# One drain of GpSimd behind the seventh expert's last output scatter, in a fused attention and mixture-of-experts kernel

## Chip, cores and metric

The kernel runs on one core of one Trainium2 chip. The metric is the device time of one execution in microseconds. The kernel before took 474.51 us, the median of three runs (473.42 to 476.02).

## What is computed

Local and global attention over 8 batches and 8 heads (512 local tokens, 32 global ones, head size 64, a window of 32 to either side) gives 4352 token rows of 512 floats. A mixture of 8 experts follows: each row whose skip score is positive goes to the expert with the highest gate value, and the expert's output, times its gate weight, is added to the row. Rows that are not computed stay as they are.

```python
x = attn_out.transpose(0, 2, 1, 3).reshape(B * S, H * D)   # 4352 x 512
do_compute = x @ w_skip > 0
xc = x[do_compute]
e_idx = argmax(xc @ w_gate, axis=1)
gate_w = softmax(xc @ w_gate)[range(len(xc)), e_idx]
for e in range(E):                                         # 8 experts
    mask = e_idx == e
    h = maximum(xc[mask] @ w1[e], 0.0)                     # 512 -> 1024
    y[mask] = gate_w[mask, None] * (h @ w2[e])             # 1024 -> 512
out[do_compute] = xc + y
```

## The kernel before, in words

The first part (to about 235 us) is the attention, 32 pairs of heads in a hand-written order. It writes each finished row to `out` in DRAM, computes the routing, and with indirect DMAs that GpSimd issues (line 688) it scatters row number and gate weight into a list `lst` with one stretch for each expert.

The second part is the loop `for e in range(E)` at line 1041, unrolled, one turn for each expert. The order of the instructions on TensorE, VectorE, ScalarE, GpSimd and SyncE is the program's own (`tc.manual_schedule`, line 1014), so each engine takes its instructions in the order in which the code gives them. A turn for expert e, as far as GpSimd is in it:

- Line 1043: two indirect DMAs (line 119, in `gather`) fetch the expert's rows 256 to 511 from `out` into the tile `xmore`. They are issued whether there are that many rows or not. Then, for e from 1 to 6, two more (line 1049) fetch the first 256 rows of expert e+1 into `xfirst` or `xsecond`.
- Line 1078, `ffn`: 256 rows through both matrix products on TensorE. For the first 128 rows VectorE adds gate weight times result to the row (line 1007, tile `yo`) and GpSimd scatters them into `out` (line 1008, in `put`). The second 128 rows are kept back.
- Lines 1054 and 1083: each engine loads the expert's row count into a register and branches. Only where the count is over 256 are the rows in `xmore` computed. On the way around, the engines bring the semaphores up to what the skipped instructions would have made them; GpSimd does this for those of its DMAs with an instruction that the trace names INC_SWDGE_SEM.
- Line 1104, `leave()`: the second 128 rows are finished (line 1007, tile `ylast`) and scattered (line 1008).

In the unrolled program expert 7 (e = 7) is the last. The two gathers at its head, its two scatters and its branch are all that GpSimd issues behind the last scatter of expert 6. Behind the loop the framework closes the kernel; those instructions stand under line 1163 in the trace: SyncE waits for the semaphores one after the other, each engine executes an instruction named DRAIN and posts a semaphore, GpSimd waits for these posts, releases the engines, clears semaphores and drains again, and a second exchange of semaphores ends the program. Line 1153 holds the matching opening. Sequencer instructions (those whose engine name ends in q in the trace) do not count as busy time of an engine.

Of the kernel before, what the change touches and what calls it, by code (L numbers as in the profile page):

```python
# [25 lines left out]
E, F = 8, 1024  # L26
# [18 lines left out]
def kernel(  # L45
# [12 lines left out]
    nc = tc.nc  # L58
# [42 lines left out]
    def index(es, g):  # L101
        nc.vector.tensor_copy(six[:, es, g], lt[:, es, g, :, 0])

    def slots(es, g):
        if g == 0:
            nc.sync.dma_start(
                lt[:, es, 0].rearrange("p e t c -> p e (t c)"),
                l3[es, 0:GRP, :].rearrange("e (p t) c -> p e (t c)", t=NSUB),
            )
        else:  # L110
            for t in range(NSUB):
                nc.sync.dma_start(
                    lt[:, es, 1, t],
                    l3[es, GRP + t * P:GRP + (t + 1) * P, :].rearrange("e p c -> p e c"),
                )

    def gather(xg, gidx, nrow=NT):
        for t in range(NSUB):
            ins = nc.gpsimd.indirect_dma_start(  # L119
                out=xg[:, t, :], out_offset=None, in_=out[0:nrow, :],  # L120
                in_offset=bass.IndirectOffsetOnAxis(ap=gidx[:, t:t + 1], axis=0),
                bounds_check=nrow - 1, oob_is_err=False,
            )
            apart(ins, "gathers", "scatters")
# [3 lines left out]
    def tick(n=1):  # L128
        for _ in range(n):
            if stages:  # L130
                stages.pop(0)()

    def send_some(n):
        for _ in range(n):
            if sends:
                sends.pop(0)()
# [7 lines left out]
    def load_piece(e, eng=nc.sync):  # L144
        mine = raws.setdefault(e, {})
        i = len(mine)
        if i == PIECES:
            return
        at = (e - 1) * PIECES + i
        pool = early if e == 0 or at % 6 < 2 else stage  # L150
        raw = mine[i] = pool.tile([P, WC], F32, tag="raw", name="raw")
        j = i % (PIECES // 2)
        if i < PIECES // 2:
            eng.dma_start(raw, w1[e, j * P:(j + 1) * P, :])
        else:
            k = WC // DM
            eng.dma_start(
                raw.rearrange("p (c n) -> p c n", n=DM),
                w2[e, j * k * P:(j + 1) * k * P, :].rearrange("(c p) n -> p c n", p=P),
            )  # L160

    class Weights:
# [19 lines left out]
        def split(self, eng, parts=1):  # L182
            if self.done < parts * self.n:
                i, k = divmod(self.done, parts)
                self.done += 1
                sl = slice(k * WC // parts, (k + 1) * WC // parts)
                hi, lo, raw = self.view(i, "h")[:, sl], self.view(i, "l")[:, sl], self.raw[i][:, sl]
                nc.scalar.copy(hi, raw)
                eng.tensor_sub(lo, raw, hi.bitcast(F32))
# [11 lines left out]
    def turn_x(xg, i, nt=NSUB, bank=ps_t):  # L201
        xh, xl = xs[i]
        for t in range(nt):
            pt = bank("xt")
            for c in range(NC):
                nc.tensor.transpose(  # L206
                    pt[:, c * P:(c + 1) * P], xg[:, t, c * P:(c + 1) * P], ident
                )
            p3 = pt.rearrange("p (c n) -> p c n", n=P)
            ts_ = slice(t * P, (t + 1) * P)  # L210
            step = NC if nt > 1 else NC // 2
            for c in range(0, NC, step):
                nc.scalar.copy(xh[:, c:c + step, ts_], p3[:, c:c + step])  # L213
            nc.vector.tensor_sub(xl[:, :, ts_], p3, xh[:, :, ts_].bitcast(F32))
        return xh, xl
# [4 lines left out]
    with ExitStack() as actx:  # L220
# [549 lines left out]
        with tc.manual_schedule(engines=engines):  # L770
# [19 lines left out]
            for u in range(NU + 2):  # L790
# [73 lines left out]
                def after():  # L864
                    if u == NU - 2:
                        send_some(len(sends))
                        slots(first, 0)
                    if u == NU - 1:
                        tick(len(stages))
# [144 lines left out]
    with tc.manual_schedule(engines=engines | {mybir.EngineType.SP}):  # L1014
        def load_weights(e):
            weights[e] = Weights(e, *((w1b, w1b, w2b) if e % 2 else (w1a, v1a, w2a)))

        xgs = [xfirst, xsecond]
        x2 = x2[0]
        tick(13)  # L1020

        PARTS = [(slice(1, 2), 0), (slice(0, 1), 1), (slice(2, E), 0), (slice(1, E), 1)]

        def lists():
            send_some(len(sends))
            for es, g in PARTS:
                slots(es, g)
            nc.vector.tensor_sub(cnt, base[0:1, :], base0[0:1, :])
            nc.vector.tensor_copy(cni, cnt)  # L1029

        def rest():
            for es, g in PARTS[:2]:
                index(es, g)
            gather(xsecond, six[:, 1, 0, :])
            gather(xmore, six[:, 0, 1, :])
            for _ in range(4):
                weights[1].load(nc.gpsimd)
            for _ in range(2):
                load_piece(2, nc.gpsimd)

        for e in range(E):
            if e:
                gather(xmore, six[:, e, 1, :])
            if e + 1 < E:
                load_weights(e + 1)
                for _ in range(8 if e else 2):
                    weights[e + 1].load()
                if e:
                    gather(xgs[(e + 1) % 2], six[:, e + 1, 0, :])

            num, x2n = [], []

            def nxt():
                num.append(nc.values_load(cni[0:1, e:e + 1], min_val=0, max_val=CAP))  # L1054
                if e + 1 < E:
                    x2n.append(turn_x(xgs[(e + 1) % 2], (e + 1) % 2))

            def split():
                if e + 1 < E:
                    weights[e + 1].split(nc.vector)  # L1060

            if e == 0:
                todo = {i: split for i in (4, 5, 6, 7)}
                def after():
                    tick(len(stages))
                    lists()

                def others():
                    for es, g in PARTS[2:]:
                        index(es, g)  # L1070

                todo.update({1: after, 9: rest, 16: others, 22: nxt})
            else:
                todo = {i: lambda e=e: weights[e].split(nc.vector) for i in range(4)}
                todo.update({i: split for i in (4, 5, 6, 8)})
                todo[16] = nxt

            leave = ffn(
                e, x2, xgs[e % 2], lambda t, e=e: lt[:, e, 0, t, 1:2], six[:, e, 0, :],
                lambda i: todo.get(i, int)(), ps_v,  # L1080
            )
            num = num[0]
            with tc.If(num > GRP):  # L1083
                more = (
                    xmore, lambda t, e=e: lt[:, e, 1, t, 1:2], six[:, e, 1, :],
                )
                with tc.If(num > GRP + P) as big:  # L1087
                    ffn(e, turn_x(xmore, e % 2), *more)()
                    with tc.If(num > 2 * GRP):
                        with tc.For_i(2 * GRP, num, GRP) as i:  # L1090
                            lt2 = fw.tile([P, NSUB, 2], F32, name="lt2", bufs=1)
                            nc.sync.dma_start(
                                lt2.rearrange("p t c -> p (t c)"),
                                l3[e, ds(i, GRP), :].rearrange("(p t) c -> p (t c)", t=NSUB),
                            )
                            s2 = fw.tile([P, NSUB], U32, name="s2", bufs=1)
                            nc.vector.tensor_copy(s2, lt2[:, :, 0])
                            gather(xmore, s2)
                            ffn(
                                e, turn_x(xmore, e % 2), xmore, lambda t: lt2[:, t, 1:2], s2,  # L1100
                            )()
                with big.Else():
                    ffn_half(e, turn_x(xmore, e % 2, 1), *more)
            leave()
            x2 = x2n[0] if x2n else None


_INS = ["qT", "kT", "v", "vgl", "qgT", "w9", "w1", "w2"]
# [58 lines left out]
```

## Time and profile before

| what | us |
|---|---|
| median of three runs | 474.51 |
| range of these runs | 473.42 to 476.02 |
| the profiled execution's own time | 475.83 |
| its span, first to last instruction | 474.1 |
| granted TensorE clock, mean share of full speed | 0.975 |

TensorE is busy for 442.0 us of the span, VectorE for 303.2, ScalarE for 284.1 and GpSimd for 231.1. Times in the rows below count from the start of the span. A busy time of an engine leaves out the instructions that its sequencer handles alone, so a stretch in which no engine is busy has to be looked up among the sequencer instructions of a line.

### The profile page before, as it was taken

What the parts mean: (1) busy time and instruction counts of PE and PEld (TensorE: products, weight loads), DVE (VectorE), ACT (ScalarE), POOL (GpSimd) and SP (SyncE); (2) the same over time, 40 slices, a digit from 0 to 9 for tenths busy, and PEclk for the clock granted to TensorE, in tenths of its full rate; (3) what the DMA queues carried; (4) which work ended last, traced back from release to release, by engine and by line L of the source; (5) the groups of instructions that cost most, each with busy time, mean ns of one, the idle gap of its engine ahead of it and who ended that gap; (6) DMA issues with size and microseconds to landing.
All of it is one profiled execution on the core that took longest, in us unless ns stands there. A gap on an engine that the chain in (4) does not pass through costs nothing. (4 is left out here: it accounts for less than half of the span.)

```text
span 474.1 us, 13569 instructions
## 1 busy us (share of the span) xinstructions
PE 442.0 (93%) x4962; PEld 373.8 (79%) x4962; DVE 303.2 (64%) x1207; ACT 284.1 (60%) x867; POOL 231.1 (49%) x238
## 2 busy tenths in 40 slices
PE   8799999998899999799989999999999999999991
PEld 4677878786788777689869797989779898698980
DVE  6898888997778789866433184848317575166610
ACT  5699999998899988664412081818126272254500
POOL 7567777789966778874461050505005140042300
PEclk9799999999999999979989999999999999999997
DMA  7989998989998896413546056565604857037000
GB/s 257 294 295 320 300 314 313 304 303 295 294 272 259 199 319 159 133 47 99 104 103 243 24 187 239 178 255 179 252 1 145 301 166 295 3 119 246 25 18 17
DMA packets 50593, 93.32 MB, mean 197 GB/s; under 512 B 15644, under 2 KB 19996, under 8 KB 50496
## 3 DMA queue, kind: packets, MB, share of 16 engines
q1 hardware_dynamic: 44384, 80.78, 53.5%
q0 software_dynamic: 6112, 11.30, 7.1%
q8 instruction: 55, 0.90, 0.9%
q14 instruction: 42, 0.34, 0.3%
HBM read 82.91 MB, written 14.67 MB: 206 GB/s over the span
## 5 line engine op out<-in xcount | busy, mean ns | idle before, releaser
L398 ACT ACTIVATE prob<-prob,nmx 128x160 f32<-128x160 f32 x256 | 106.8, 423 | 15.4 <-DVE nmx L393 15.3
L435 POOL TENSOR_TENSOR prob<-prob,inv 128x640 f32<-128x640 f32 x64 | 80.6, 1261 | 33.1 <-DVE inv L431 18.3
L1008 POOL DMA_INDIRECT out_dram<-yo,six x12 | 12.2, 1017 | 126.8 <-DVE yo L1007 109.3
L931 ACT ACTIVATE hh<-ph 128x256 fp32r<-128x256 f32 x72 | 27.6, 384 | 66.8 <-PE ph L926 62.9
L942 PE MATMUL py<-w2h,hlw 128*128 128x512 f32 x144 | 56.6, 393 | 0.5 <-DVE hlw L932 0.5
L942 PE MATMUL py<-w2h,hh 128*128 128x512 f32 x144 | 57.0, 396 | 0.0
L942 PE MATMUL py<-w2l,hh 128*128 128x512 f32 x144 | 56.4, 392 | 0.0
L380 PE MATMUL pss<-ks,qs 64*64 64x160 f32 x1024 | 53.4, 314 | 0.9 <-DVE nmx L393 0.5
L398 ACT ACTIVATION_READ_ACCUMULATOR prob<-prob,nmx 128x1 f32 x256 | 49.5, 193 | 0.0
L539 PEld LDWEIGHTS pv<-ptT,vw 128*64 128x64 f32 x1024 | 41.9, 140 | 9.2 <-issue 8.6
L926 PE MATMUL ph<-xh,w1h 128*128 128x256 f32 x288 | 46.1, 282 | 2.5 <-ACT xh L213 0.8
L539 PE MATMUL pv<-ptT,vw 128*64 128x64 f32 (+1 forms) x1024 | 46.7, 240 | 0.0
L926 PE MATMUL ph<-xh,w1l 128*128 128x256 f32 x288 | 45.4, 280 | 0.0
L926 PE MATMUL ph<-xl,w1h 128*128 128x256 f32 x288 | 45.4, 280 | 0.0
L932 DVE SCALAR_TENSOR_TENSOR hlw<-ph,hh 128x256 fp32r<-128x256 f32 x72 | 30.2, 420 | 20.7 <-ACT hh L931 19.9
L380 PEld LDWEIGHTS pss<-ks,qs 64*64 64x64 f32 x1024 | 35.8, 138 | 9.4 <-issue 5.5
L926 PEld LDWEIGHTS ph<-xh,w1h 128*128 128x128 f32 x288 | 39.0, 189 | 4.9 <-issue 3.7
L688 POOL DMA_INDIRECT lst<-dat,slu x34 | 34.7, 1022 | 15.0 <-DVE cni L1029 6.3
L213 ACT CAST xh<-xt 128x512 fp32r<-128x512 f32 (+1 forms) x22 | 11.2, 551 | 50.2 <-PE xt L206 50.2
L476 PE MATMUL pst<-ident,prob 128*128 128x128 f32 x256 | 40.7, 286 | 0.0
L926 PEld LDWEIGHTS ph<-xl,w1h 128*128 128x128 f32 x288 | 38.8, 189 | 0.0
L926 PEld LDWEIGHTS ph<-xh,w1l 128*128 128x128 f32 x288 | 38.7, 189 | 0.0
(178 smaller groups left out, 970.2 us busy)
## 6 DMA issues: line engine op xcount, KB each, us to landing
raw<-in_w_dram SPq DMA_DIRECT2D x58, 512.0 KB, 6.1
vw<-in_v_dram SPq DMA_DIRECT2D x32, 512.0 KB, 7.1
ks<-in_kT_dram SPq DMA_DIRECT2D x32, 400.0 KB, 5.7
out_dram<-xr SPq DMA_DIRECT2D x32, 256.0 KB, 5.8
qs<-in_qT_dram SPq DMA_DIRECT2D x31, 256.0 KB, 5.9
raw<-in_w_dram POOLq DMA_DIRECT2D x6, 512.0 KB, 5.7
vgs<-in_vgl_dram SPq DMA_DIRECT2D x32, 64.0 KB, 5.5
lst<-dat,slu POOLq DMA_INDIRECT x34, 5.3
```

The costliest lines, as they stand in the source:

```text
L213: nc.scalar.copy(xh[:, c:c + step, ts_], p3[:, c:c + step])
L380: nc.tensor.matmul(banks[odd][head(h ^ odd), j * W:(j + 1) * W], q[head(h), w * QB:(w + 1) * QB], window(k[head(h)], w), start=True, stop= ...
L398: nc.scalar.activation(pt[:, i, :], pt[:, i, :], AF.Exp, bias=nmx[:, i:i + 1], scale=-1.0, accum_out=sums[:, i, 0:1],)
L435: nc.gpsimd.tensor_mul(pt[:, sl, :], pt[:, sl, :], inv[:, sl].unsqueeze(2).to_broadcast([P, 4, W]),)
L476: nc.tensor.transpose(pst[:, i * P:(i + 1) * P], pt[:, 4 * hf + i, 0:KW], ident)
L539: nc.tensor.matmul(pv[head(h), j * 96:j * 96 + n], vv[:, w, head(h)], ptT[:, w, h ^ odd, 0:n], start=False, stop=j == 3, skip_group_check= ...
L688: ins = nc.gpsimd.indirect_dma_start(out=lst, out_offset=bass.IndirectOffsetOnAxis(ap=slu[:, t:t + 1], axis=0), in_=dat[:, bs[j], t - 4 * ...
L926: nc.tensor.matmul(ph[:, 0:GRP], hl[a][:, c, f * P:(f + 1) * P], bb[:, c, :], start=i == 0, stop=i == 3 * NC - 1,)
L931: nc.scalar.activation(hh[:, f, :], ph[:, 0:GRP], AF.Relu)
L932: nc.vector.scalar_tensor_tensor(hlw[:, f, :], ph[:, 0:GRP], 0.0, hh[:, f, :].bitcast(F32), ALU.max, ALU.subtract,)
L942: nc.tensor.matmul(py, a[:, f, ts_], hl[bb][:, f, :], start=f == 0 and i == 0, stop=f == NF - 1 and i == 2,)
L1008: ins = nc.gpsimd.indirect_dma_start(out=out, out_offset=bass.IndirectOffsetOnAxis(ap=sidx, axis=0), in_=yo, in_offset=None, bounds_check= ...
```

## The change

One instruction is added to the loop over the experts: behind `leave()` of the turn with e = 6, GpSimd executes a drain. Nothing else differs.

```diff
             leave()
             x2 = x2n[0] if x2n else None
+            if e == E - 2:
+                nc.gpsimd.drain()
```

In GpSimd's order the drain stands between the scatter of `ylast` of expert 6 (line 1008) and the first gather of `xmore` of expert 7 (line 119).

## Rows read from the trace of the kernel before

**Rows 1.** The page: the span.
```profile
span 474.1 us, 13569 instructions
```
**Rows 2.** Sums by stretch: length, busy time (instructions) by engine, granted clock, DMA share, GB/s.
```profile
446.40:459.20 12.80, 12.80 (x84) 11.62 (x83) 5.83 (x10) 3.44 (x7) 0.00 (x0) 1.00 0.01 2
...
465.70:474.10 8.40, 0.00 (x0) 0.00 (x0) 0.00 (x0) 0.00 (x0) 0.00 (x0) 0.59 0.06 21
```
**Rows 3.** Timeline, 463 us to the end: start, length, engine, operation, idle before it.
```profile
463.23 0.39 PE L942 MATMUL py<-w2h,hlw 128*128 128x512 f32 x1
463.66 0.75 DVE L1007 SCALAR_TENSOR_TENSOR ylast<-py,lt,xsecond 128x512 f32<-128x512 f32 x1 [4.69 <-PE py L942]
464.69 1.00 POOL L1008 DMA_INDIRECT out_dram<-ylast,six  x1 [4.42 <-DVE ylast L1007]
```
**Rows 4.** Line 1008, the last scatter (464.69): issue to landing.
```profile
DMA to landing us min/median/max: 2.6/2.6/2.6
```
**Rows 5.** Line 1163 by time, 463 us on: ns min/median/max, first and last start.
```profile
L1163 DVEq DRAIN  x1: 791/791/791, 463.7 to 463.7; - x1
L1163 PEldq DRAIN  x1: 8/8/8, 463.8 to 463.8; - x1
L1163 POOLq DRAIN  x1: 8833/8833/8833, 464.5 to 464.5; - x1
...
L1163 SPq EVENT_SEMAPHORE  x9: 28/28/28, 467.3 to 467.8; - x9
L1163 SPq DRAIN  x2: 7/10/13, 467.9 to 467.9; - x2
...
L1163 POOLq EVENT_SEMAPHORE  x4: 17/17/17, 473.3 to 474.0; - x4
L1163 POOLq DRAIN  x2: 46/78/109, 473.5 to 473.9; - x2
```
**Rows 6.** The chain that ended last, its last piece: start, length, what.
```profile
464.45 1.24 POOLq L1163
```
**Rows 7.** GpSimd's semaphore instruction on the way around a branch, five of eight.
```profile
L1089 POOLq INC_SWDGE_SEM  x1: 1182/1182/1182, 273.0 to 273.0; - x1
...
L1083 POOLq INC_SWDGE_SEM  x1: 1266/1266/1266, 291.2 to 291.2; - x1
...
L1083 POOLq INC_SWDGE_SEM  x1: 1406/1406/1406, 315.0 to 315.0; - x1
...
L1083 POOLq INC_SWDGE_SEM  x1: 1930/1930/1930, 436.3 to 436.3; - x1
...
L1083 POOLq INC_SWDGE_SEM  x1: 2011/2011/2011, 460.1 to 460.1; - x1
```
**Rows 8.** DMA issues of GpSimd (POOLq), all of them: count, median us to landing.
```profile
raw<-in_w_dram POOLq DMA_DIRECT2D x6, 512.0 KB, 5.7
...
lst<-dat,slu POOLq DMA_INDIRECT x34, 5.3
...
xmore<-out_dram,six POOLq DMA_INDIRECT x16, 3.6
...
out_dram<-yo,six POOLq DMA_INDIRECT x12, 3.4
xfirst<-out_dram,six POOLq DMA_INDIRECT x8, 5.5
xsecond<-out_dram,six POOLq DMA_INDIRECT x8, 6.6
out_dram<-ylast,six POOLq DMA_INDIRECT x8, 2.7
```
**Rows 9.** Line 1153, the opening of the program: GpSimd's drain before any DMA.
```profile
L1153 POOLq DRAIN  x1: 183/183/183, 0.4 to 0.4; - x1
```
**Rows 10.** Timeline of GpSimd, 440 us on, without its last scatter.
```profile
442.07 1.00 POOL L1008 DMA_INDIRECT out_dram<-ylast,six  x1 [5.31 <-DVE ylast L1007]
443.37 1.05 POOL L119 DMA_INDIRECT xmore<-out_dram,six  x1 [0.30 <-issue]
444.73 1.63 POOL L119 DMA_INDIRECT xmore<-out_dram,six  x1 [0.31 <-issue]
459.25 1.02 POOL L1008 DMA_INDIRECT out_dram<-yo,six  x1 [12.89 <-DVEq L1083]
```
**Rows 11.** Line 1008, the scatter at 442.07: issue to landing.
```profile
DMA to landing us min/median/max: 2.8/2.8/2.8
```
**Rows 12.** Tile xmore, 430 us to the end: every instruction that touches it.
```profile
L119 POOL DMA_INDIRECT xmore<-out_dram,six x2: 1052/1339/1626, 443.4 to 444.7; - x2
```
**Rows 13.** Line 119, all gathers to 441 us: ns of one, and landing.
```profile
L119 POOL DMA_INDIRECT xmore<-out_dram,six x14: 994/1122/1636, 243.1 to 424.7; - x14
...
DMA to landing us min/median/max: 2.2/4.4/7.8
```

## Prediction

> **What bounds the kernel now.** I began with the page's span, 474.1 us [rows 1], and asked which work ends it. Up to 463 us it is TensorE: behind its last matmul at 463.23 VectorE finishes the last 128 rows at 464.41, and GpSimd issues their scatter from 464.69 to 465.69 [rows 3]. The scatter lands 2.6 us after its start, at 467.3 [rows 4]. After that nothing of the computation is left, yet the span goes on to 474.1: in the 8.4 us from 465.7 no engine is busy at all [rows 2]. A stretch like that has to be looked up among the sequencer instructions, and the chain of work names the line: its last piece is GpSimd's sequencer on line 1163, from 464.45 [rows 6].
>
> The instructions of that line, in order of time, are the heart of this case [rows 5]. The drains of TensorE and VectorE take 8 and 791 ns and are over by 464.5. SyncE has its last wait released by the landing at 467.3, steps through nine short waits, and its two drains begin at 467.9. GpSimd's drain takes 8833 ns: 464.45 + 8.83 = 473.28. The exchange of semaphores that ends the program starts at 473.3 and takes 474.1 - 473.3 = 0.8 us. So of the 6.8 us behind the landing, SyncE's steps explain 0.6 and the exchange 0.8. The 5.3 us between 467.9 and 473.3 belong to GpSimd's drain alone, with everybody else done.
>
> **Why that drain is long.** Three rows say what a drain costs when little stands before it: 183 ns at the opening, before any DMA [rows 9], and 109 and 46 ns for the two that follow the long one in the same closing [rows 5]. So a drain has no fixed price of 9 us. Nor is it the wait for the last transfer: it outlasts the landing by 473.28 - 467.3 = 5.98 us.
>
> The trace holds a second instruction whose length shows the same kind of growth. INC_SWDGE_SEM takes 1182 ns at 273 us, 1266 at 291, 1406 at 315, 1930 at 436 and 2011 at 460 [rows 7]. I set these against the DMAs that GpSimd has issued before each. All its issues are 6 + 34 + 16 + 12 + 8 + 8 + 8 = 92 [rows 8]; the last one comes behind the INC at 460, which so has 91 before it. Counting back through the program's order gives 87 at 436 us, 61 at 315, 55 at 291 and 49 at 273. The steps are 84 ns for 6, 140 for 6, 524 for 26 and 81 for 4: about 20 ns for each DMA in the last three, 829 / 42 = 19.7 over all. Time is not what it follows: 291 to 315 and 436 to 460 are both 23.8 us long, and the growth is 140 and 81 ns, with 6 and 4 DMAs. So in GpSimd's bookkeeping every DMA since the program's start still stands as an entry, though nearly all landed long ago, and some work of GpSimd's walks over them. The line's foot is 1182 - 49 x 19.7 = 217 ns.
>
> My reading is that a GpSimd drain settles those entries one by one and leaves the list empty. The price of an entry in a drain has two ends. If the walk over 92 begins with the landing it is 5.98 / 92 = 65 ns; if it begins behind the scatter's issue at 465.69 it is 7.59 / 92 = 83 ns. That the next drain takes 109 ns fits a list that was emptied.
>
> **The change, part by part.** It adds one instruction and removes and moves none.
>
> The added drain stands behind the scatter of expert 6, the one at 442.07 [rows 10], which leaves 92 - 4 = 88 entries (two gathers and two scatters come after it). From the scatter's landing, 442.07 + 2.8 = 444.87 [rows 11], 88 x 65 ns = 5.7 us give 450.6; from its issue end, 443.07, 88 x 83 ns = 7.3 us give 450.4. I take 450.6. Its shortest bound is the landing itself, 444.9; its longest comes from the load of the other engines, which the closing did not have: the second gather of `xmore` takes 1.63 us where the shortest takes 0.99 [rows 10, 13], a factor of 1.6, and 443.07 + 1.6 x 7.3 = 454.8.
>
> Queued behind it on GpSimd are the two gathers of `xmore` of expert 7, then the scatter at 459.25. The gathers now run from 443.15 to 446.36, 3.3 us behind the scatter's end; behind the drain they end at 450.6 + 3.3 = 453.9. What hides this is GpSimd's idle time: 12.89 us before the scatter at 459.25 [rows 10], in which TensorE is busy throughout [rows 2] and which ends with data from VectorE. There remain 459.25 - 453.9 = 5.3 us, and 1.1 us at the long bound. Nobody misses the gathers: after 430 us no instruction but the gathers themselves touches `xmore`, since expert 7 has no more than 256 rows [rows 12]. They must have landed before GpSimd goes around the branch, just before the INC at 460.1 [rows 7]: with the shortest landing, 2.2 us [rows 13], from the second one's start at 450.6 + 1.7 = 452.3, that is 454.5, and with the longest, 7.8 us, 460.1, a little late for the branch and 4 us ahead of the last scatter. SyncE has loads neither before nor behind in this stretch (2 GB/s are moved [rows 2]). Cost of the added drain: nothing.
>
> In the turn of expert 7 the INC_SWDGE_SEM at 460.1 finds 3 entries and not 91: about 217 + 3 x 20 = 0.28 us in place of 2.01. It gains nothing, since the last scatter waits for VectorE until 464.41 [rows 3].
>
> At the end, the framework's drain finds 4 entries. Behind the landing at 467.3 it needs 4 x 65 ns = 0.26, or, if it walked before, next to nothing: it ends between 467.3 and 467.6. Then SyncE is last, at 467.94, with its nine waits behind the same landing [rows 5]. The exchange, with about 0.05 to pass the signal, takes 0.85 us: 467.94 + 0.85 = 468.8. **The sum:** span 474.1 - 468.8 = 5.3 us less.
>
> The profiled execution took 475.83 us, 1.7 more than its span, and lies 1.3 above the median. What is saved lies inside the span, so I take it from each: 475.8 - 5.3 = 470.5 for that execution, 474.51 - 5.3 = **469.2** for the median.
>
> **What the Trainium skill says against it.** The row shows 8833 ns for GpSimd's drain in the closing and 7.6 us of it with the engine idle [rows 2, 5]. The Trainium skill, "PSUM — Partial Sum Buffer", section "Engine vs sequencer instructions", says that a drain waits for the engine to go fully idle, and names nothing else. By that rule alone the closing's drain would have ended at 465.7, and one more drain would save nothing. The trace disagrees by 7.6 us, but how entries are kept is told in no row, so the rule stands as the first rival below.
>
> **The rivals.** *The length does not depend on what is outstanding, or the drain does not empty the list.* The 5.98 us would be a price of the closing itself, paid again. For it: only one long drain is in the trace, and none is seen in the middle of work. Against it: the three short drains, and the line of INC_SWDGE_SEM. The added drain would then hide in the 12.89 us, as above, even at 8.83 us: 474.5. Here also belongs a drain that does not do what it says.
>
> *Part of it.* The drain is rid of the walk that INC_SWDGE_SEM shows, 92 x 20 ns = 1.8 us, and the other 4.1 us stay: 474.51 - 1.8 = 472.7, within 0.5%.
>
> *Slower: the drain outlasts its cover.* The place is GpSimd's queue from the drain to the last scatter. Behind the drain stand 3.3 us of gathers, 1.3 of the scatter of `yo` and its gap, and 2.0 of the INC [rows 7, 10]: 6.6 us. The last scatter waits for VectorE until 464.4, so it moves once the drain ends after 457.8, that is, after 14.7 us, twice the walk of 7.3. For it: GpSimd's work stretches under VectorE's load, by up to 1.6. Against it: 1.6 gives 454.8, and the gain in the closing would have to be lost as well. A drain of 20 us that empties nothing would end at 463.1 and give 474.5 + 5.3 = 479.8.
>
> **How the numbers follow.** Full gain 0.79 (469.2), part 0.05 (472.7), no effect 0.12 (474.5), slower 0.04 (479.8). Measurement tells about 0.5%, or 2.4 us, from no change. The full gain is 1.1%, so faster has 0.80 with a little of the partial cases, same 0.16, slower 0.04. For the range I take the full gain with the spread of the runs before, 1.1 below their median and 1.5 above, 468.1 to 470.7, and stretch it to the partial case, 472.7. It leaves out no effect and slower.
>
> **What would show it.** Right: a DRAIN of GpSimd of 7 to 9 us near 442 to 451, the gathers at about 451, INC_SWDGE_SEM at 460 of about 0.3 us, the closing's drain of about 3 us that ends with the landing, and SyncE's drain as the last before the exchange. Wrong: an INC still near 2 us (the list was not emptied), a closing drain still ending 6 us behind the landing, or the scatter of `yo` later than 459.3 (the cover did not hold).

## The result and the profile after

The changed kernel takes 468.26 us (median of four runs, 467.36 to 469.02) where the kernel before takes 474.45 beside it: ratio 0.9847, 95% interval [0.9812, 0.9882]. With 474.45 us that is 467.2 us, faster by 7.2 us or 1.5%. (The ratio is the comparison's own estimate and not the quotient of the two medians, which is 0.9870, or 6.2 us.) Forecast were 469.2 us and a gain of 5.3. The profiled execution took 467.36 us, with this span:

```profile
span 465.6 us, 13570 instructions
```

First the end of the timeline, as in [rows 3] (start, length, engine, operation, idle before it), and the last scatter's landing [rows 4]:

```profile
460.02 0.39 PE L942 MATMUL py<-w2h,hlw 128*128 128x512 f32 x1
460.44 0.75 DVE L1007 SCALAR_TENSOR_TENSOR ylast<-py,lt,xsecond 128x512 f32<-128x512 f32 x1 [4.69 <-PE py L942]
461.48 1.00 POOL L1008 DMA_INDIRECT out_dram<-ylast,six  x1 [4.42 <-DVE ylast L1007]
...
DMA to landing us min/median/max: 2.6/2.6/2.6
```

From the last matmul to the scatter nothing has changed but the place on the clock: all of it comes 3.2 us earlier than before. Then the closing, the line that was 1163 and is 1165 now, as in [rows 5], with the added drain (line 1107) ahead of it (ns min/median/max, first and last start):

```profile
L1107 POOLq DRAIN  x1: 8508/8508/8508, 438.7 to 438.7; - x1
...
L1165 POOLq DRAIN  x1: 3064/3064/3064, 461.2 to 461.2; - x1
...
L1165 SPq EVENT_SEMAPHORE  x9: 27/28/28, 464.1 to 464.6; - x9
L1165 SPq DRAIN  x2: 7/10/13, 464.7 to 464.7; - x2
...
L1165 POOLq EVENT_SEMAPHORE  x4: 17/17/17, 464.8 to 465.5; - x4
L1165 POOLq DRAIN  x2: 46/78/109, 464.9 to 465.3; - x2
```

GpSimd's closing drain has shrunk from 8.83 to 3.06 us. It ends at 461.24 + 3.06 = 464.30, 0.2 us behind the landing at 464.1, and SyncE, with its nine waits, is now the last, at 464.7. The exchange starts at 464.8. The long drain has not vanished: it stands at 438.7 and lasts 8.5 us. GpSimd's timeline shows what covers it, in the places of [rows 10]:

```profile
438.90 1.00 POOL L1008 DMA_INDIRECT out_dram<-ylast,six  x1 [5.31 <-DVE ylast L1007]
448.09 1.05 POOL L119 DMA_INDIRECT xmore<-out_dram,six  x1 [8.19 <-issue]
449.45 1.01 POOL L119 DMA_INDIRECT xmore<-out_dram,six  x1 [0.31 <-issue]
456.03 1.02 POOL L1008 DMA_INDIRECT out_dram<-yo,six  x1 [5.58 <-DVEq L1083]
```

The gathers wait 8.19 us where they waited 0.30, and the scatter behind them still has 5.58 us to spare of the 12.89 before. GpSimd's semaphore instruction, just ahead of the drain and behind it [rows 7]:

```profile
L1083 POOLq INC_SWDGE_SEM  x1: 1930/1930/1930, 433.1 to 433.1; - x1
...
L1083 POOLq INC_SWDGE_SEM  x1: 251/251/251, 456.9 to 456.9; - x1
```

It falls from 1930 to 251 ns with the drain between the two; before, it went on to 2011. The drain has emptied what that instruction walks over.

So the difference of the two spans, 474.12 - 465.56 = 8.56 us, has two parts. From the start of the last matmul to the end of the span it was 474.12 - 463.23 = 10.89 us and is 465.56 - 460.02 = 5.54 (I call this the closing): 5.35 us. The other 3.21 us, up to the last matmul (the head), had been gained before the drain was reached: the scatter in front of it already came 3.17 us earlier (438.90 and 442.07). The forecast knew only the first part.

### The profile page after: what moved, and what is told of

It reads as the page before. It is cut to its first block, busy times and chain, and to the rows that moved or that the text cites. A ratio compares the mean times of both kernels' runs of the same rounds, so it can differ in the third digit from the quotient of the medians.

```text
span 465.6 us, 13570 instructions
## 1 busy us (share of the span) xinstructions
PE 435.7 (94%) x4962; PEld 368.9 (79%) x4962; DVE 302.5 (65%) x1207; ACT 283.3 (61%) x867; POOL 231.6 (50%) x238
## 5 line engine op out<-in xcount | busy, mean ns | idle before, releaser
L380 PE MATMUL pss<-ks,qs 64*64 64x160 f32 x1024 | 50.9, 304 | 1.4 <-DVE nmx L393 1.1
L380 PEld LDWEIGHTS pss<-ks,qs 64*64 64x64 f32 x1024 | 34.2, 132 | 8.7 <-issue 5.2
L476 PE MATMUL pst<-ident,prob 128*128 128x128 f32 x256 | 39.7, 281 | 0.0
```

The source lines that it names most:

```text
L380: nc.tensor.matmul(banks[odd][head(h ^ odd), j * W:(j + 1) * W], q[head(h), w * QB:(w + 1) * QB], window(k[head(h)], w), start=True, stop= ...
L476: nc.tensor.transpose(pst[:, i * P:(i + 1) * P], pt[:, 4 * hf + i, 0:KW], ident)
```

## The experiments

Ratios are against the kernel before on the same chip in the same rounds. The first four runs below share one chip (before: 473.90 us, 29 runs). The drain behind expert 5, the one early drain, the first run with a drain in every turn and the last run of this section share a second (480.83, 20 runs). The pair that is timed side by side has a third (481.54, 11 runs).

**The kernel before, again.** Nothing is edited. It asks whether the 3.2 us of the head belong to the change.

> The kernel before, unchanged, timed against itself and profiled a second time. Theory (the gain lies wholly behind the last scatter; the 3.2 us by which the changed kernel's profile was ahead before its drain are the spread of executions): ratio 1.000, its closing drain again 8.8 us, last matmul to end of span again 10.9 us, while the times of the head rows (at 248 us, at 386 us, the last matmul at 463.2) move by 1 to 3 us between this profile and the first. Rival (the added instruction shifts something ahead of the drain): the second profile repeats the first one's times to within 0.5 us up to the last matmul, 463.2.

Ratio 1.0009 [0.9988, 1.0031]. Its second profile has a span of 471.0 us, 3.1 less than the first:

```profile
460.09 0.39 PE L942 MATMUL py<-w2h,hlw 128*128 128x512 f32 x1
...
L1163 POOLq DRAIN  x3: 46/109/8835, 461.3 to 470.7; - x3
```

The same program reaches its last matmul at 460.09 in one execution and at 463.23 in another, while its closing drain repeats to 2 ns. The 3.2 us of the head need no drain, then: executions of one program differ by as much. Sums by stretch show part of what differs, the clock that TensorE is granted. In the first profile it is 0.50, the lower of its two levels (1.2 GHz), from 13.3 to 20.1, 201.1 to 207.8 and 245.5 to 248.8 us, some 17 us ahead of the last matmul; in the second from 200.0 to 206.8 alone, and in the changed kernel's from 18.0 to 21.3 alone. Both rows are 13.3 to 20.1 us, first of the first profile, then of the second (length, busy time and instructions by engine, granted clock, DMA share, GB/s):

```profile
13.30:20.10 6.80, 5.76 (x59) 4.45 (x59) 6.61 (x30) 3.53 (x15) 4.56 (x5) 0.50 1.03 343
```

```profile
13.30:20.10 6.80, 4.66 (x85) 3.69 (x87) 6.73 (x34) 3.29 (x15) 4.10 (x4) 1.00 1.00 340
```

Of the 3.1 us, 1.0 is there by 66 us and 3.0 by 249 us.

**The change, again.** Nothing is edited.

> The changed kernel again, five rounds. Theory (only the closing is shortened): 474.5 - 5.35 = 469.1 us, ratio 0.9887; drain behind expert 6 8.5 us, closing drain 3.1 us. Rival (a further gain ahead of the drain that the change brings, as the first comparison's ratio of 0.9847 suggests): 467.2 us, ratio 0.985.

468.32 us, ratio 0.9899 [0.9868, 0.9931]. The closing is 5.55 us, the drains 8505 and 3070 ns. The interval takes in the 0.9887 of the closing alone and leaves out the 0.985 of the rival. Span less closing gives the head of every execution, if each has the closing of the profiles: 461.42 us on the mean of these five (standard deviation 1.26), 461.53 for the 29 of before (1.14).

**An instruction without effect in the drain's place.**

```diff
             if e == E - 2:
+                nc.gpsimd.nop()
```

> In the drain's place an instruction that does nothing, so that GpSimd's program has the same length and the same order as in the changed kernel. Theory (the drain's walk over the outstanding DMAs is what counts): no change, 474.5 us, ratio 1.000, INC_SWDGE_SEM at 460 us 2.01 us, closing drain 8.8 us. Rival (length or layout of GpSimd's program brings part of the gain): ratio 0.996 to 0.998, 1 to 2 us less than before, with an unchanged closing.

Ratio 0.9995 [0.9977, 1.0013]; INC_SWDGE_SEM at 460.6 takes 2011 ns and the closing drain 8835. The trace shows no instruction on that line, and 13569 in all as before, so this says nothing about length: it is one more run of the kernel before. That other added instructions bring no such gain is shown by the next run.

**Twelve more DMAs, without the drain.** GpSimd copies the small tile first8 twelve times into unused DRAM, in its idle time.

```diff
+    spare = dram.tile([12, P, E], F32, name="spare")
 ...
             if e:
                 gather(xmore, six[:, e, 1, :])
+            if e == E - 1:
+                for k in range(12):
+                    nc.gpsimd.dma_start(spare[k], first8)
```

> The kernel before, without the drain, with 12 more small DMAs that GpSimd issues from the tile first8 into unused DRAM at the head of expert 7's turn, in its idle time. Theory (the closing drain walks over every DMA since the start, 82.6 ns each, from the last scatter's issue on): INC_SWDGE_SEM at 460 us 2.01 + 12 x 0.020 = 2.25 us; the closing drain ends 104 x 82.6 ns = 8.59 us behind the last scatter's issue where it was 7.60, so the span grows by 0.99 us: 475.5 us, ratio 1.002. Rival (a fixed price of the closing): 7.60 us again, 474.5 us.

```profile
461.14 0.39 PE L943 MATMUL py<-w2h,hlw 128*128 128x512 f32 x1
...
L1087 POOLq INC_SWDGE_SEM  x1: 2223/2223/2223, 458.0 to 458.0; - x1
...
L1167 POOLq DRAIN  x3: 46/109/9810, 462.4 to 472.7; - x3
```

The drain grows from 8833 to 9810 ns, 81 ns for each DMA, and the closing from 10.89 to 473.01 - 461.14 = 11.87 us, by 0.98 where 0.99 was expected. INC_SWDGE_SEM grows by 212 ns, 18 for each. The DMAs themselves were issued from 444.3 to 450.7 us and landed within 2.9 us each, so they were over by 454; what is paid is their number. The time, with a ratio of 1.0018 [0.9999, 1.0037], agrees with 1 us and could not show it alone.

**The drain one turn earlier, behind expert 5.**

```diff
-            if e == E - 2:
+            if e == E - 3:
                 nc.gpsimd.drain()
```

> The same drain one turn earlier, behind expert 5's last scatter, where the gathers of the next expert's rows stand behind it. Theory (the drain costs nothing only where GpSimd has cover): in the profile's clock the walk over 82 entries takes 82 x 82.6 = 6.8 us from the scatter's issue, and the four gathers behind it start 6.7 us later; those of xsecond, which landed 0.8 us before TensorE's transposes of it (434.4 and 435.2 before), land 2 to 6 us after that point, and TensorE stands still for so long. Closing 5.5 us as in the changed kernel, since 10 entries are left. Sum 474.0 - 5.3 + 2 to 6 = 470.7 to 474.7 us. Rival (any place does as well): 468.6 us and no idle time of TensorE before the transposes.

GpSimd's timeline and TensorE's transposes of that turn:

```profile
424.35 1.04 POOL L1008 DMA_INDIRECT out_dram<-ylast,six  x1 [1.75 <-issue]
433.63 2.10 POOL L119 DMA_INDIRECT xmore<-out_dram,six  x1 [8.24 <-issue]
436.03 1.01 POOL L119 DMA_INDIRECT xmore<-out_dram,six  x1 [0.31 <-issue]
437.35 1.00 POOL L119 DMA_INDIRECT xsecond<-out_dram,six  x1 [0.30 <-issue]
438.65 1.00 POOL L119 DMA_INDIRECT xsecond<-out_dram,six  x1 [0.30 <-issue]
...
450.08 1.00 POOL L1008 DMA_INDIRECT out_dram<-ylast,six  x1 [9.10 <-DVE ylast L1007]
...
440.72 0.63 PE L206 MATMUL xt<-ident,xsecond 128*128 128x128 f32 x4 [2.84 <-DMA xsecond<-out_dram,six]
441.97 0.66 PE L206 MATMUL xt<-ident,xsecond 128*128 128x128 f32 x4 [0.62 <-DMA xsecond<-out_dram,six]
```

The same drain, 8.6 us long, is now in front of gathers that TensorE waits for: it stands still for 2.84 and 0.62 us at the head of its transposes. Behind this its granted clock falls to 0.50 from 442.7 to 446.1 us, where nine matmuls start 0.43 us apart and the ones behind them 0.23:

```profile
442.70:446.10 3.40, 3.40 (x9) 2.64 (x8) 0.69 (x1) 0.55 (x1) 0.00 (x0) 0.50 0.02 7
```

So the turn costs more than the waits. From expert 5's last scatter to expert 6's it takes 450.08 - 424.35 = 25.73 us; in the kernel before the first of them stands here and the second at 442.07 [rows 10], 20.27 us later:

```profile
421.80 1.04 POOL L1008 DMA_INDIRECT out_dram<-ylast,six  x1 [1.75 <-issue]
```

That is 5.46 us more: 3.46 of it are the waits, and about 1.8 (an estimate, nine times 0.20) goes with the lower clock. The closing is 5.55 us as in the changed kernel, 5.35 less than before, so by the trace nothing of the gain is left. Measured are 0.9974 [0.9934, 1.0014], or 1.2 us less with an interval that takes in no gain. The drain's place decides, not the drain.

**One drain early, under cover.**

```diff
                     gather(xgs[(e + 1) % 2], six[:, e + 1, 0, :])
+                if e == 1:
+                    nc.gpsimd.drain()
```

> One drain behind the gathers of expert 1's turn, in GpSimd's idle time before the scatter of that turn. Theory: 54 entries are settled there, hidden (it must wait for the gathers' landing, 5.4 us, too); INC_SWDGE_SEM at 291 falls from 1.27 to about 0.2 us. 38 DMAs follow it, so the closing drain ends 38 x 82.6 = 3.14 us behind the last scatter's issue, which is 0.9 us later than SyncE's last wait lets it in the changed kernel: closing about 6.4 us from the last matmul where the kernel before has 10.9 and the changed one 5.5; time 474.0 - 4.5 = 469.5. Rival (the closing's price is fixed, or a drain settles only recent DMAs): closing near 10.9 or near 5.5.

```profile
L1051 POOLq DRAIN  x1: 12434/12434/12434, 287.9 to 287.9; - x1
...
L1085 POOLq INC_SWDGE_SEM  x1: 223/223/223, 301.8 to 301.8; - x1
...
L1085 POOLq INC_SWDGE_SEM  x1: 931/931/931, 470.1 to 470.1; - x1
...
L1165 POOLq DRAIN  x3: 46/109/4451, 474.5 to 479.5; - x3
```

Ratio 0.9890 [0.9845, 0.9935], forecast 469.5 / 474.0 = 0.9905. The list is empty behind the drain (223 ns) and fills again, to 931 ns at 470. The closing is 6.53 us: 38 entries cost 1.0 us that 4 do not. TensorE has no new wait near 300 us although this drain, which also waits for the gathers, stands for 12.4.

**A drain in every turn, under cover, and beside it the change.** Behind the gathers of each turn from expert 1 on:

```diff
+            if e:
+                nc.gpsimd.drain()
             num, x2n = [], []
```

> A drain behind the gathers of every turn from expert 1 to 7, each in GpSimd's idle time; looks for a version better than the changed kernel. Theory (the walks of INC_SWDGE_SEM and the waits for landing are off TensorE's path): every INC_SWDGE_SEM about 0.2 to 0.3 us, closing 5.5 us, time as the changed kernel's, 468.5, within 0.5 us. Rival (the shorter INC brings the next turn's gathers forward and TensorE gains): 467 us. Third possibility (a drain waits for landings of up to 7.8 us and delays a scatter or the next turn): over 469.5 us, with idle time of TensorE before its transposes.

> The changed kernel, on the same chip and in the same rounds as the kernel with a drain in every turn. Theory (both shorten the closing to 5.5 us and nothing else): ratio 0.989, closing 5.5 us; the two kernels' ratios agree within their intervals.

> The kernel with a drain behind the gathers of every turn, beside the changed kernel. Theory: ratio 0.989 as the changed kernel's, closing 5.5 us, since the walks of INC_SWDGE_SEM that it shortens by up to 1.8 us are off TensorE's path. Rival (they are on it): ratio 0.985 or less, 2 us below the changed kernel.

On the second chip the drain in every turn has 0.9881 [0.9841, 0.9921]; side by side on the third it has 0.9852 [0.9822, 0.9883] and the change 0.9858 [0.9824, 0.9892], 474.50 and 474.58 us. Each INC_SWDGE_SEM behind the first drain takes 208 to 223 ns, up to 1.8 us less than before, and nothing is seen to come of it. The two medians cannot tell 2 us apart, but the profiles can: from the first expert's last scatter to the last matmul they take 187.1 and 187.2 us with a drain in every turn and 186.6 to 187.5 with the change. Those walks are off TensorE's path. The closing is 5.54 us in all three profiles. No version here beats the change.

**The change with the twelve DMAs behind the drain.**

> The changed kernel with the 12 small DMAs of the earlier run at the head of expert 7's turn, behind the drain. Theory (82.6 ns for each entry, from the last scatter's issue, beside the wait for the landing): 16 entries take 1.32 us, less than the 1.6 us to the landing, so the closing stays at 5.5 us from the last matmul and the time at 468.5, where the same DMAs cost the kernel before 0.97 us of closing. Rival (the entries are settled behind the landing): 0.8 to 1.0 us more, closing 6.0 to 6.5 us.

0.9909 [0.9873, 0.9945], closing 5.73 us; the closing drain takes 3567 ns, 0.50 more than in the changed kernel. Neither expectation holds: the drain grows by half of what the rival had and not by nothing. The closing hardly feels it, since SyncE is still last: its drain ends 3.43 us behind the start of the last scatter (3.25 in the changed kernel), GpSimd's 3.33. With the 12 DMAs the wait that the landing releases stands first in SyncE's row, so that twelve waits, 0.06 us apart, follow the landing and not nine; that is the 0.19 us.

## Why the prediction was right, and where it was wrong

**What bounds the end** was right. GpSimd's drain was the last thing in the closing with everybody else done; with it short, SyncE's nine waits are last, as the sum had put it. The forecast end, 468.8, less the 3.2 us of the head is 465.6, the measured span.

**That the drain pays for entries, and that a drain removes them**, was read from INC_SWDGE_SEM and from the short drains. The changed kernel shows the emptying (251 ns, forecast 280), the twelve DMAs the price of each, the early drain the refilling. A price fixed for the closing, the first rival, falls with them, and with it the rule of the Trainium skill ("PSUM — Partial Sum Buffer", section "Engine vs sequencer instructions") taken as the whole price: the added drain ends 7.3 us behind the issue of the scatter in front of it, with no other work on GpSimd.

**The price of an entry** was mis-sized in form, without harm. I had two ends, 65 ns behind the landing and 83 ns behind the issue, as if one of them were true. Put side by side, the end of the drain behind the last scatter's issue (length of the drain less 1.24 us, since it starts 0.24 before the scatter and that takes 1.00) is:

| entries | 2 | 4 | 10 | 16 | 38 | 92 | 104 |
|---|---|---|---|---|---|---|---|
| us | 1.74 | 1.83 | 2.08 | 2.33 | 3.21 | 7.60 | 8.57 |

From 2 to 38 this is 41 ns for each entry, from 92 to 104 it is 81. The landing comes 1.62 us behind the issue. One form fits all seven of these closing drains to 0.06 us: the longer of 41 ns for each entry and the landing, and then 41 ns for each entry once more. It looks like two passes, the first of which runs beside the transfer; that is a reading of lengths, and nothing shows the passes themselves. The drain behind expert 5 needed 7.3 us for 82 entries and not my 6.8. The same form gives 7.2 if the scatter there landed as late as in the kernel before, 4.9 us behind its start; its landing in that run is not shown.

**The cover** was right: the gathers of the last turn delay nobody, and the scatter behind them keeps 5.6 us. The gathers were forecast for 451 us and come at 448.1 in a profile that is 3.2 us ahead, which is 451.3. The drain behind expert 5 is the counter-proof: the rival of an uncovered drain has its mechanism, in another place than I had put it, and with a price of 5.5 us that takes the whole gain back.

**What failed is the range**, in the step on how the numbers follow: its lower end, 468.1, took the spread of three runs of before, 1.1 us below their median, as all that a comparison can differ by. The first comparison's 0.9847 gives 467.2 us, 0.9 below it (the median of the changed kernel's four runs, 468.26, lies just inside). The size of the one term in the sum was not at fault (5.3 forecast, 5.35 in the closing). What was missing is that the head of this kernel spreads by about 4 us from run to run (459.9 to 464.1 over 29 executions): with a standard deviation of 1.1 us, the means of two samples of four can differ by 1.6 us on their own, as an estimate of twice the standard error. The 1.9 us by which 7.2 exceeds the closing's 5.35 are of about that size, and the larger comparison does not repeat them: luck of the samples, as far as these runs show, and no gain. The profiled execution of before, 475.8 us, also lay high in that spread, as its distance of 1.3 us to the median told. The comparison with 29 runs gives 0.9899, or 469.7 us, 0.5 from the forecast.

What makes the head spread was argued nowhere in the prediction, and no run sets it. The profiles show one thing that goes with it. In the four of the first chip the clock is granted at half for 13.7, 10.2, 6.8 and 3.4 us ahead of the last matmul, which comes at 463.8, 461.1, 460.1 and 460.4; in the first pair of profiles it is 17.1 and 3.4 us, and 463.2 and 460.0. That the clock is the cause is a reading and not shown.

One thing stays open. On the third chip the heads of the change average 467.7 us (six executions, standard deviation 1.9) and those of the drain in every turn 467.4 (six, 1.5) against 469.2 (eleven, 1.3), 1.5 and 1.8 us less; on the first chip the difference was 0.1, and on the second the change with twelve DMAs had 468.3 against 468.3. That is about twice the uncertainty, and no run here shows a way in which a drain could act on the time ahead of it. Behind the added drain nothing differs: from the scatter in front of it to the last matmul the change's three profiles take 21.1 to 21.2 us, and so do those of the kernel before.

## What to carry to other kernels

Look at the sequencer instructions behind the last useful transfer: a program that issues many DMAs from GpSimd can pay for their number once, at its end, in a drain that no busy time shows. An earlier drain moves that price to where GpSimd has nothing to do, and it helps only there: check what stands behind it in GpSimd's order and who waits for that. Few entries may stay for the end, as long as the drain over them ends before the steps of the others behind the last landing, as it did here with 4 and with 16.

## What was not expected

- A drain's price in entries fits 41 ns each behind the landing and 41 more each beside it, over closing drains of 2 to 104 entries.
- Waits of 2.8 and 0.6 us cost TensorE more than themselves: behind them its clock was granted at half for 3.4 us.
- The closing repeats to 0.01 us between profiles (10.89 and 10.90 without a drain, 5.54 and 5.55 with one late in the loop, on three chips), while the head varies by 4 us.
- The mean granted clock of an execution, 0.975 before and 0.996 after, mixes two things. About 0.007 of the difference is the closing: TensorE is idle behind its last matmul, and in the kernel before the clock there is granted at half, the lower of its two levels, 1.2 GHz, for the last 6.8 us. The rest, 0.014, is the head with its 17.1 and 3.4 us at half. The first row is before, 6.7 us behind the landing; the second is the changed kernel, where the closing ends before much of that:

```profile
467.40:474.10 6.70, 0.00 (x0) 0.00 (x0) 0.00 (x0) 0.00 (x0) 0.00 (x0) 0.50 0.00 0
```

```profile
462.50:465.60 3.10, 0.00 (x0) 0.00 (x0) 0.00 (x0) 0.00 (x0) 0.00 (x0) 0.92 0.15 58
```
